# A spectral filter beside a 32-head attention: the filter's last stage computed for 321 of 640 columns, GpSimd joining the mirrored rest, and a planner that knows GpSimd's exclusion

## The chip, the cores and the metric

The program runs on one core of one Trainium2 chip. The metric is the device time of one execution in microseconds (us); the runs of the kernel before took 755.43, 756.69 and 756.99 us.

## What is computed

Two independent blocks on bf16 inputs; their outputs stand side by side (2048 rows, 640 + 640 columns).

```python
def _A_ref(x, w_r, w_i):            # x: 1 x 2048 x 640
    X = rfft2(x.astype(float32), axes=(-2, -1))      # 2048 x 321
    X = X * (w_r + 1j * w_i)
    return irfft2(X, s=(2048, 640)).astype(bfloat16)

def _B_ref(x, wqkv, wo):            # 32 heads of 20
    q, k, v = heads(x @ wqkv)
    p = softmax(q @ k.T * 20 ** -0.5)
    return (p @ v) @ wo
```

## The kernel before, in words

**Attention** has 32 units (512 queries by 4 heads), each of 64 score tiles of 128 x 512, 2048 tiles in all. TensorE (PE) writes score tiles to PSUM banks (L817). A tile then takes one of two ways:

- Two tiles at a time go to ScalarE (ACT), which takes the exponential of 1024 columns in one instruction (L1444).
- Four tiles make a batch for VectorE (DVE): it clamps each tile out of PSUM to an integer (`p1`, L972, one tile or two), and makes two shifted copies of the batch in SBUF (`p2`, L1020, and `p3`, L1019, 2048 columns each). The exponential is the sum of three terms. GpSimd (POOL) scales the value tile for one of them (`vs`, L1029; on DVE, L1031, before the folding below is done).

PE then multiplies with the values (`pv`, L1102): 4 matmuls for 4 tiles of ACT, 12 for a batch of DVE. At the end of a unit the sums are inverted and sent round through DRAM, and POOL normalises (`onorm`, L1154). The projections are L620, L649 and L698, transposes of the input L598, the output product L1248 and L1253. At the start DVE copies four padded weight blocks (`padw`, L559), without which the first projections cannot run, while POOL fills constants with memsets (L566 to L572).

**The filter** works on rows folded by symmetry. POOL folds the input early (`fold`, L1659 to L1666). Then PE runs four stages of matmuls in the gaps of the attention: S1 (L1772), S2 (L1855), S3 (L1959) and S4 (L2011), with DVE taking results out of PSUM. S4 makes the output: for each of 8 blocks of 128 rows, two halves of 320 columns and two sets T, six matmuls of 320 columns sum cosine and sine parts in one bank; DVE copies set 0 to `T1` (L2019) and adds and subtracts set 1 (L2030, twice) into the rows `s` and `s + 1024`, which are stored.

**The order** of every engine's instructions is fixed when the program is built. The class `KB` plays the program through with a price for each instruction (the numbers beside each operation, such as `exp_occ`), and writes down what each engine takes next: `try_act_fill` and `dve_fill` share the score tiles out between ACT and DVE as each comes free, `try_bg` puts projection and filter jobs into PE's gaps, `pick_dve` chooses DVE's next operation, `step_aux` POOL's and the DMA queue's. Filter jobs have release times that are spread between `FT0` = 200 us and `FT1` = 700 us in proportion to PE's price of the jobs ahead. `keep_warm` adds a dummy matmul (L1536) where PE would idle. On the chip the engines run these fixed orders and wait for each other by semaphores. In `put`, a DVE operation `p2` or `p3` that is begun while POOL is busy costs 44% of the overlap more.

## Time and profile before

| | |
|---|---|
| runs, median of 3 | 756.69 us (755.43 to 756.99) |
| profiled execution, first to last instruction | 759.9 us |
| PE / DVE / ACT / POOL busy | 722.7 / 678.2 / 723.8 / 206.7 us |
| exponentials on ACT | 774 of 1024 columns |
| mean granted TensorE clock | 0.994 |

The profiled execution has no other time of its own than its span; it lies 3.2 us over the median of the runs. Busy times of PE come from pipelined matmuls with modelled ends, so they say little of how near PE is to its peak. For ACT and DVE the busy share can be read as it stands.

### The profile page before, as it was taken

What the parts mean: (1) busy time and instruction counts of PE and PEld (TensorE: products, weight loads), DVE (VectorE), ACT (ScalarE), POOL (GpSimd) and SP (SyncE); (2) the same over time, 40 slices, a digit from 0 to 9 for tenths busy, and PEclk for the clock granted to TensorE, in tenths of its full rate; (3) what the DMA queues carried; (4) which work ended last, traced back from release to release, by engine and by line L of the source; (5) the groups of instructions that cost most, each with busy time, mean ns of one, the idle gap of its engine ahead of it and who ended that gap; (6) DMA issues with size and microseconds to landing.
All of it is one profiled execution on the core that took longest, in us unless ns stands there. A gap on an engine that the chain in (4) does not pass through costs nothing.

```text
span 759.9 us, 16458 instructions
## 1 busy us (share of the span) xinstructions
PE 722.7 (95%) x6520; PEld 232.3 (31%) x6565; DVE 678.2 (89%) x1172; ACT 723.8 (95%) x787; POOL 206.7 (27%) x253
## 2 busy tenths in 40 slices
PE   8998999999999999999999999999999999999997
PEld 4422232332322222232223323322222232333333
DVE  3599999989989899999989988999899999999895
ACT  5899999999999999999999989999999999999994
POOL 7296952111211022122331123212121222122110
PEclk9999999999999999999999989999999999999999
DMA  9023321202102116213120112103010012111101
GB/s 314 11 72 90 96 71 52 48 20 49 34 21 57 42 46 222 76 37 104 38 53 16 47 37 51 24 21 110 20 44 22 16 46 84 38 45 48 51 23 56
DMA packets 43503, 44.68 MB, mean 59 GB/s; under 512 B 16740, under 2 KB 36582, under 8 KB 43166
## 3 DMA queue, kind: packets, MB, share of 16 engines
q1 hardware_dynamic: 42654, 42.25, 18.9%
q0 software_dynamic: 768, 1.32, 0.7%
q8 instruction: 54, 0.88, 0.5%
q14 instruction: 27, 0.22, 0.1%
HBM read 28.47 MB, written 8.36 MB: 48 GB/s over the span
## 4 chain that ended last, share of the span: by engine, by line
PE 51%; ACT 38%; DVE 9%; issue 2%; DVEq 0%
ACT arena L1444 37%; PE ps L817 18%; PE ps L1102 14%; PE ps L649 5%; DVE arena L972 3%; PE ps L698 3%; PE ps L1855 3%; PE ps L1772 2%; DVE arena L1019 2%; PE ps L1248 2%; PE ps L2011 2%; PE ps L1959 2%; DVE arena L1020 1%; PE ps L620 1%; PE ps L578 1%
## 5 line engine op out<-in xcount | busy, mean ns | idle before, releaser
L1444 ACT ACTIVATE arena<-ps 128x1024 f16<-128x1024 f32 x774 | 716.6, 1092 | 17.6 <-PE ps L817 11.2
L972 DVE TENSOR_SCALAR arena<-ps 128x512 int16<-128x512 f32 (+1 forms) x490 | 330.8, 692 | 31.8 <-PE ps L817 30.4
L817 PE MATMUL ps<-arena 32*128 32x512 bf16 x2048 | 304.9, 386 | 13.6 <-ACT arena L1444 10.0
L1102 PE MATMUL ps<-arena 128*32 128x512 f16 x3048 | 240.9, 386 | 4.4 <-DVE arena L1019 2.1
L817 PEld LDWEIGHTS ps<-arena 32*128 32x128 bf16 x2048 | 75.1, 91 | 285.9 <-ACT arena L1444 255.9
L1029 POOL TENSOR_SCALAR arena<-arena 128x96 bf16<-128x96 bf16 x112 | 74.5, 669 | 250.6 <-PE ps L1102 245.7
L1019 DVE TENSOR_SCALAR arena<-arena 128x2048 int16<-128x2048 int16 x125 | 93.7, 750 | 5.5 <-PE ps L1102 5.1
L1154 POOL TENSOR_TENSOR arena<-arena 128x512 bf16<-128x512 f32 x30 | 40.6, 1353 | 204.8 <-DMA arena<-rd 204.7
L1020 DVE TENSOR_SCALAR arena<-arena 128x2048 int16<-128x2048 int16 x125 | 92.9, 743 | 1.5
L1102 PEld LDWEIGHTS ps<-arena 128*32 128x32 bf16 x3048 | 52.3, 94 | 104.2 <-issue 70.2
L649 PE MATMUL ps<-arena 128*128 128x512 bf16 x149 | 45.7, 383 | 4.2 <-issue 2.4
L1855 PE MATMUL ps<-arena 128*128 128x322 bf16 (+1 forms) x198 | 39.2, 311 | 3.3 <-DVE arena L1904 1.8
L2011 PE MATMUL ps<-arena 128*128 128x320 bf16 (+1 forms) x192 | 35.7, 302 | 0.1
L698 PE MATMUL ps<-arena 128*128 128x160 bf16 x320 | 32.2, 234 | 1.0 <-DVE arena L972 1.0
L1887 DVE TENSOR_TENSOR arena<-ps,arena 128x644 bf16<-128x644 f32 (+1 forms) x34 | 27.9, 821 | 4.1 <-PE ps L1855 2.3
L1959 PE MATMUL ps<-arena 128*128 128x512 bf16 (+3 forms) x123 | 29.9, 333 | 1.3 <-issue 1.3
L1248 PE MATMUL ps<-arena 128*128 128x320 bf16 (+1 forms) x152 | 28.2, 302 | 0.2 <-DVE arena L1887 0.2
L1133 DVE COPY arena<-ps 128x512 f32<-128x512 f32 (+1 forms) x33 | 22.0, 669 | 5.9 <-PE ps L1102 5.6
L698 PEld LDWEIGHTS ps<-arena 128*128 128x128 bf16 x320 | 21.1, 98 | 14.7 <-issue 11.1
L661 DVE TENSOR_SCALAR arena<-ps 128x512 bf16<-128x512 f32 x34 | 23.1, 678 | 0.1
L1772 PE MATMUL ps<-arena 128*128 128x512 bf16 x72 | 21.7, 383 | 1.0 <-issue 0.8
L1855 PEld LDWEIGHTS ps<-arena 128*128 128x128 bf16 (+1 forms) x198 | 14.9, 98 | 21.6 <-issue 10.8
(83 smaller groups left out, 369.9 us busy)
## 6 DMA issues: line engine op xcount, KB each, us to landing
arena<-rd SPq DMA_DIRECT2D x120, 64.0 KB
out_dram<-arena SPq DMA_DIRECT2D x32, 160.0 KB
arena<-in_A_x_dram SPq DMA_DIRECT2D x16, 160.0 KB
xs<-arena SPq DMA_DIRECT2D x16, 160.0 KB
arena<-xs SPq DMA_DIRECT2D x4, 640.0 KB
arena<-arena SPq DMA_DIRECT2D x105, 20.0 KB
arena<-ct SPq DMA_DIRECT2D x2, 1024.0 KB
arena<-ct SPq DMA_DIRECT2D x4, 512.0 KB
```

Source lines behind the costliest of these rows:

```text
L649: return lambda e: e.matmul(o, l, r_, start=(cc == 0), stop=(cc == 4))
L698: return lambda e: e.matmul(o, l, r_, start=st, stop=(c == 4), skip_group_check=True)
L817: return e.matmul(self.ps[:, bank, :], self.KT[32 * j:32 * j + 32, g, kt * 128:(kt + 1) * 128], self.QT[32 * j:32 * j + 32, g, qc * 512:(q ...
L972: return e.tensor_scalar(o, in_, 0.0, 31744.0, ALU.max, ALU.min)
L1019: self.dve_push([(lambda e, en: e.tensor_scalar(Ii, Ii, SH2, 0.0, ALU.subtract, ALU.max), occ, ik + pk, ik, [], "p3")], lambda: push(self. ...
L1020: ops = [(lambda e, en: e.tensor_scalar(Gi, Ii, SH1, 0.0, ALU.subtract, ALU.max), occ, ik, [("G", b)], [], "p2")]
L1029: self.pool_op(lambda e: e.tensor_scalar(vs, vi, W1, None, ALU.mult), 300.0, r=vr, w=vk, name="vs")
L1102: inst = e.matmul(self.ps[32 * j:32 * j + 32, bank, :], v_, p_, start=s_, stop=False, tile_position=(0, 32 * j), skip_group_check=True)
L1444: self.put("act", lambda e: e.activation(o, in_, AF.Exp, bias=ACT_BIAS, scale=ACT_SCALE), 0.8333 * 512 * n + 60.0, r=[("ps", b) for b in b ...
L1855: return lambda e: e.matmul(o, lhs, r_, start=st, stop=sp)
L1959: return lambda bank: (lambda e: e.matmul(ps[0:M, bank, lo_:hi_], l, rhs, start=st, stop=sp, skip_group_check=True))
L2011: return lambda e: e.matmul(o, l, r_, start=(n == 0), stop=(n == 5))
```

## The change

Four things are changed at once.

1. **S4.** Cosine sums (m = 0) and sine sums (m = 1) go to banks of their own, for columns 0 to 320 alone (`FBC` = 322 with padding). Three matmuls of 322 columns fill a bank instead of six of 320: 96 matmuls in place of 192. DVE's operations keep their number (16 copies to `T1`, 32 adds and subtracts) at 322 columns, but write f32 buffers `uw`. The columns from 321 to 639 mirror 319 to 1: there the cosine sum is the same and the sine sum has the other sign.
2. **join.** Four new POOL operations for each of the 8 row blocks: cosine plus sine for columns 0 to 320, cosine minus sine read backwards for 321 to 639, for each of two rows. 32 in all; the stores follow them.
3. **The planner's exclusion.** `plock` holds, for POOL and DVE, the end of the last operation of the list `PORT`. An operation of the list on one of the two starts, in the plan, only after that of the other has ended; `pick_dve` passes such an operation over if POOL holds the lock for over 100 ns more. The 44% rule is gone.
4. **Prices.** `exp` 913 to 905 ns for two tiles, `p2`/`p3` 632 to 600, `vs` 300 to 430, `onorm` 1600 to 1250, `fold` 1600, 1500, 440, 860, 1160 to 1360, 1460, 275, 820, 815.

```diff
-        if eng == "dve" and name in ("p2", "p3", "p4") and self.free["pool"] > st:
-            occ += min(self.free["pool"] - st, 1.8 * occ) * 0.44
+        port = name in self.PORT
+        if port and eng == "dve":
+            st = max(st, self.plock["pool"])
+        if port and eng == "pool":
+            st = max(st, self.plock["dve"])
         end = st + occ
+        if port:
+            self.plock[eng] = end
...
+    PORT = {"p2", "p3", "vs", "S2.evL", "padw", "onorm", "fold", "ms_vp", "ms_v1", "ms_k", "ms_q", "x24z", "wpad", "wz", "ms_sb", "join"}
...
+            if op[5] in self.PORT and self.plock["pool"] > self.now + 100.0:
+                continue
...
-        return 0.8333 * 512 * n + 60.0
+        return 0.8333 * 512 * n + 52.0
...
-            for half in range(2):
+            b2 = sc % 2
+            for m in range(2):
                 for T in range(2):
                     pe = []
-                    for n in range(6):
-                        lt, m = divmod(n, 2)
+                    for lt in range(3):
...
-                            r_ = self.G[0:M, lt, m, half * 320:(half + 1) * 320]
-                            return lambda e: e.matmul(o, l, r_, start=(n == 0), stop=(n == 5))
+                            r_ = self.G[0:M, lt, m, :]
+                            return lambda e: e.matmul(o, l, r_, start=(lt == 0), stop=(lt == 2))
...
+                                return lambda e, en: e.tensor_tensor(self.uw[b2][m][sgn], self.T1, ps[:, bank, 0:FBC], op)
...
+    def join(self, sc, b2):
+        za = ("z", "A", 3)
+        for sgn in range(2):
+            c, n = self.uw[b2][0][sgn], self.uw[b2][1][sgn]
+            y = self.yo[sgn]
...
+            self.pool_op((lambda y, c, n: lambda e: e.tensor_tensor(y[:, 0:321], c[:, 0:321], n[:, 0:321], ALU.add))(y, c, n), 817.0, r=r, w=[("ys", sc, sgn, 0)], name="join")
+            self.pool_op((lambda y, c, n: lambda e: e.tensor_tensor(y[:, 321:640], c[:, 319:0:-1], n[:, 319:0:-1], ALU.subtract))(y, c, n), 817.0, r=r, w=[("ys", sc, sgn, 1)], name="join")
```

The planner makes another order of the whole program from this. Lines of the changed kernel stand 10 to 15 lower (L1444 is L1456 there, L817 is L827, L2011 is L2025). Three places of the two orders follow; "x774" is a count of equal instructions in a row.

ACT's whole order before, from its first copy of a transposed block to the end of the attention:

```order
L604 COPY arena<-ps 128x3x256
L604 COPY arena<-ps 128x2x256
L604 COPY arena<-ps 128x3x256 x2
L604 COPY arena<-ps 128x2x256
L1444 ACTIVATE arena<-ps 128x1024 x774
```

And now:

```order
L614 COPY arena<-ps 128x3x256 x3
L614 COPY arena<-ps 128x2x256
L714 CAST arena<-ps 128x2x8x20
L614 COPY arena<-ps 128x3x256
L1456 ACTIVATE arena<-ps 128x1024 x782
```

Eight more exponentials stand on ACT, and so 16 score tiles fewer on DVE: its batches fall from 125 to 121, PE's `pv` matmuls from 3048 to 3016. PE's dummy matmuls rise from 32 to 47.

PE's start before, from its 11 warming matmuls to the first score tiles:

```order
L578 MATMUL ps<-arena 128x512 x11
L598 MATMUL ps<-arena 128x128 x20
L1536 MATMUL ps<-arena 128x512
L620 MATMUL ps<-arena 128x512 x10
L598 MATMUL ps<-arena 128x128 x20
L817 MATMUL ps<-arena 128x512 x4
```

And now:

```order
L588 MATMUL ps<-arena 128x512 x11
L608 MATMUL ps<-arena 128x128 x20
L630 MATMUL ps<-arena 128x512 x5
L608 MATMUL ps<-arena 128x128 x20
L630 MATMUL ps<-arena 128x512 x5
L708 MATMUL ps<-arena 128x160 x10
L630 MATMUL ps<-arena 128x512 x5
L608 MATMUL ps<-arena 128x128 x10
L827 MATMUL ps<-arena 128x512 x4
```

Ten value matmuls (L708), five more projection matmuls (L630) and ten transposes (L608) now stand ahead of the first scores. On DVE the four `padw` copies, in one row before, are apart, each behind other work.

POOL's order in the filter's last stage before (no operation of that stage is on POOL):

```order
L1029 TENSOR_SCALAR arena<-arena 128x96 x4
L1154 TENSOR_TENSOR arena<-arena 128x512
L1029 TENSOR_SCALAR arena<-arena 128x96 x5
L1154 TENSOR_TENSOR arena<-arena 128x512
```

And now, at the stage's start:

```order
L1039 TENSOR_SCALAR arena<-arena 128x96 x4
L2059 TENSOR_TENSOR arena<-arena 128x321
L2060 TENSOR_TENSOR arena<-arena 128x319
L2059 TENSOR_TENSOR arena<-arena 128x321
L2060 TENSOR_TENSOR arena<-arena 128x319
L1039 TENSOR_SCALAR arena<-arena 128x96
L1164 TENSOR_TENSOR arena<-arena 128x512
```

The joins come in fours between the `vs` operations. By the number of score tiles that PE has issued, the stage's matmuls stood between the tiles 1744 and 2035 and stand now between 1800 and 1951; S1 began at tile 823 and begins at 819, S3 ended at 1712 and ends at 1780. Between the first and last DVE add of the stage stand 16 `p2` and `p3` operations now.

## Rows read from the trace of the kernel before

**Rows 1.** The page's first two parts: busy time by engine, granted clock in 40 slices.
```profile
PE 722.7 (95%) x6520; PEld 232.3 (31%) x6565; DVE 678.2 (89%) x1172; ACT 723.8 (95%) x787; POOL 206.7 (27%) x253
...
PEclk9999999999999999999999989999999999999999
```
**Rows 2.** The page's fourth part: the chain that ended last, by engine.
```profile
PE 51%; ACT 38%; DVE 9%; issue 2%; DVEq 0%
```
**Rows 3.** Groups by line: busy us, mean ns of one | idle before, releasers.
```profile
L1444 ACT ACTIVATE arena<-ps 128x1024 f16<-128x1024 f32 x774 | 716.6, 1092 | 17.6 <-PE ps L817 11.2 <-PE ps L1102 4.6
...
L1019 DVE TENSOR_SCALAR arena<-arena 128x2048 int16<-128x2048 int16 x125 | 93.7, 750 | 5.5 <-PE ps L1102 5.1
L1020 DVE TENSOR_SCALAR arena<-arena 128x2048 int16<-128x2048 int16 x125 | 92.9, 743 | 1.5
...
L2011 PE MATMUL ps<-arena 128*128 128x320 bf16 (+1 forms) x192 | 35.7, 302 | 0.1
...
L1666 POOL TENSOR_TENSOR arena<-arena 128x319 bf16<-128x319 f32 x16 | 16.0, 1002 | 0.0
...
L2030 DVE TENSOR_TENSOR arena<-arena,ps 128x320 bf16<-128x320 f32 x32 | 15.2, 475 | 1.5 <-PE ps L2011 1.4
```
**Rows 4.** Timeline of ACT: start us, us, instruction [idle before, releaser].
```profile
13.78 14.77 ACT L1444 ACTIVATE arena<-ps 128x1024 f16<-128x1024 f32 x16 [0.48 <-PE ps L817]
29.59 5.61 ACT L1444 ACTIVATE arena<-ps 128x1024 f16<-128x1024 f32 x6 [1.04 <-PE ps L817]
37.48 8.36 ACT L1444 ACTIVATE arena<-ps 128x1024 f16<-128x1024 f32 x9 [2.28 <-PE ps L817]
...
637.24 55.10 ACT L1444 ACTIVATE arena<-ps 128x1024 f16<-128x1024 f32 x60 [0.21 <-PE ps L817]
...
739.08 8.40 ACT L1444 ACTIVATE arena<-ps 128x1024 f16<-128x1024 f32 x9
```
**Rows 5.** Timeline of PE and POOL from the start to the first scores.
```profile
8.44 0.39 PE L1536 MATMUL ps<-arena 128*128 128x512 bf16 x1 [0.60 <-ACT arena L604]
9.24 2.32 PE L620 MATMUL ps<-arena 128*128 128x512 bf16 x10 [0.40 <-ACT arena L604]
11.39 1.28 PE L598 MATMUL ps<-arena 128*128 128x128 bf16 x20
...
13.68 1.14 PE L698 MATMUL ps<-arena 128*128 128x160 bf16 x14
```
**Rows 6.** Timeline around 70 us: a `p2` beside a fold on POOL.
```profile
69.86 1.94 DVE L1020 TENSOR_SCALAR arena<-arena 128x2048 int16<-128x2048 int16 x1
69.86 1.39 POOL L1659 TENSOR_TENSOR arena<-arena 128x640 f32<-128x640 bf16 x1
...
71.86 0.62 PE L1102 MATMUL ps<-arena 128*32 128x512 f16 x8 [0.46 <-DVE arena L1020]
...
72.83 1.94 ACT L1444 ACTIVATE arena<-ps 128x1024 f16<-128x1024 f32 x2 [0.28 <-PE ps L817]
```
**Rows 7.** Timeline of DVE at 196 us: a `p2` with POOL at rest.
```profile
196.07 0.68 DVE L1020 TENSOR_SCALAR arena<-arena 128x2048 int16<-128x2048 int16 x1
```
**Rows 8.** Timeline of PE near 441 us: filter matmuls of 322 columns, and `pv`.
```profile
440.63 0.59 PE L1855 MATMUL ps<-arena 128*128 128x322 bf16 x3
...
441.48 0.61 PE L1102 MATMUL ps<-arena 128*32 128x512 f16 x8
...
444.13 0.83 PE L1102 MATMUL ps<-arena 128*32 128x512 f16 x12
...
458.40 1.00 PE L1855 MATMUL ps<-arena 128*128 128x322 bf16 x6
```
**Rows 9.** Windows of 40 us: busy PE, PEld, DVE, ACT, POOL (instructions), granted clock, DMA.
```profile
80.00:120.00 40.00, 37.77 (x375) 13.45 (x377) 37.87 (x63) 38.41 (x42) 24.47 (x28) 1.00 0.31 92
440.00:480.00 40.00, 37.29 (x299) 11.86 (x291) 33.79 (x54) 35.21 (x39) 11.57 (x12) 0.91 0.18 43
640.00:680.00 40.00, 39.70 (x381) 12.69 (x382) 38.25 (x70) 40.00 (x45) 8.21 (x11) 1.00 0.13 38
```

More of the change, by code (lines that the diff above doesn't have):

```diff
@@ L323, in __init__ @@
         self.cold = False
+        self.plock = {"pool": 0.0, "dve": 0.0}
         self.win = 0
@@ L424, in alloc_filter @@
         self.Z = a.bf(zB, 3 * 4 * 1024).rearrange("p (t m s) -> p t m s", t=3, m=4)
[L425 removed]
+        self.G = a.bf(zA, 3 * 2 * FBC).rearrange("p (t m d) -> p t m d", t=3, m=2)
         self.outB += [a.bf(o, 640) for o in (zC + 5888, zC + 7168)]
[L427 to L428 removed]
+        self.T1 = a.f32(zA + 3872, FBC)
+        self.uw = [[[a.f32(zA + 5184 + 5152 * i + 2576 * m + 1288 * s, FBC) for s in range(2)] for m in range(2)] for i in range(2)]
+        self.yo = [a.bf(zA + 15488 + 1280 * s, 640) for s in range(2)]
+        assert 15488 + 2560 <= 20608
     def at(self, t):
@@ L1153, in norm_dma @@
         pk = self.pack_keys(u - 1) if u else []
-        self.pool_op(lambda e: e.tensor_tensor(on, of, bc, ALU.mult), 1600.0, r=pk + [("bcu", u, j) for j in range(4)] + [("bc", j) for j in range(4)] + [("Of", b2)],
+        self.pool_op(lambda e: e.tensor_tensor(on, of, bc, ALU.mult), 1250.0, r=pk + [("bcu", u, j) for j in range(4)] + [("bc", j) for j in range(4)] + [("Of", b2)],
                      w=[("On",), ("Onu", u)] + al, name="onorm")
@@ L2012, in jobs_A @@
                         ks = [(z_, lt, 2 * T + m) for z_ in ("Z", "Zm", "Zr")] + [("G",), zr("A", 3), zr("B", 2), zr("D", 3)]
-                        if T == 1 and sc >= 2 and n == 0:
-                            ks += [("yout", sc - 2, 0), ("yout", sc - 2, 1)]
-                        pe.append((mk, 136.0, ks))
+                        pe.append((mk, 137.0, ks))
+                    post = None
                     if T == 0:
-                        def mkev(bank, half=half):
-                            in_ = ps[:, bank, 0:320]
-                            return lambda e, en: e.tensor_copy(self.T1[half], in_)
@@ L2020, in jobs_A, with mkev @@
-                        rk = [zr("A", 3)] + ([("yo", sc - 1, half, 1)] if sc else [])
-                        ev = [(mkev, 405.0, rk, [("T1", half), zr("A", 2)], [], False)]
-                        post = None
+                        def mkev(bank):
+                            return lambda e, en: e.tensor_copy(self.T1, ps[:, bank, 0:FBC])
+                        rk = [zr("A", 3)] + ([("uw", sc, 0)] if m else [("uw", sc - 1, 1)] if sc else [])
+                        ev = [(mkev, 402.0, rk, [("T1", sc, m), ("T1",), zr("A", 2)], [], False)]
@@ L2025, in jobs_A, with mkev, post @@
                         for sgn in range(2):
-                            def mkev(bank, half=half, sgn=sgn, sc=sc):
-                                in_ = ps[:, bank, 0:320]
-                                o = self.yo[sc % 2][sgn][:, half * 320:(half + 1) * 320]
+                            def mkev(bank, sgn=sgn, b2=b2, m=m):
                                 op = ALU.add if sgn == 0 else ALU.subtract
-                                return lambda e, en: e.tensor_tensor(o, self.T1[half], in_, op)
-                            ev.append((mkev, 408.0, [("T1", half), zr("A", 3)], [("yo", sc, half, sgn), zr("A", 2)], [("yob", sc % 2, sgn)], False))
-                        post = None
-                        if half == 1:
-                            def post(J, sc=sc):
-                                o = self.out[0]
-                                for sgn in range(2):
-                                    r0 = 128 * sc + 1024 * sgn
-                                    rows = o[r0:r0 + 128, 0:640]
-                                    self.dma(rows, self.yo[sc % 2][sgn], 163840, r=[("yo", sc, hh, sgn) for hh in range(2)] + [("yob", sc % 2, sgn)],
-                                             w=[("yout", sc, sgn)], name="st_A", is_out=True)
+                                return lambda e, en: e.tensor_tensor(self.uw[b2][m][sgn], self.T1, ps[:, bank, 0:FBC], op)
+                            rk = [("T1", sc, m), ("T1",), zr("A", 3)] + ([("ys", sc - 2, i, h) for i in range(2) for h in range(2)] if sc >= 2 else [])
+                            ev.append((mkev, 402.0, rk, [("uwk", sc, m, sgn), zr("A", 2)] + ([("uw", sc, m)] if sgn else []), [], False))
+                        if m == 1:
+                            def post(J, sc=sc, b2=b2):
+                                self.join(sc, b2)
                     add(Job("S4", 0.0, pe, ev, after=S3, post=post))
```

38 lines of the change are left out of this document (20 added, 18 removed).

## The prediction

> **What bounds the kernel now.** I read the page's busy times first, then the chain, the groups by line, and last ACT's timeline and three windows. Three engines are nearly full: PE 95%, ACT 95%, DVE 89%, POOL only 27% [rows 1]. PE's share is made of pipelined matmuls and shows no limit by itself. The chain that ended last runs over PE for 51% and ACT for 38% [rows 2], so it passes to and fro between the two. What tells them apart is ACT's own beat. In its longest unbroken row, 60 exponentials take 55.10 us [rows 4]; less the last one's 1.09 us [rows 3] that is 54.0 us for 59, or 0.915 us each. ACT's attention lasts from 13.78 us to 739.08 + 8.40 = 747.5 us [rows 4], 733.7 us. At the unbroken beat 774 exponentials need 773 x 0.915 + 1.09 = 708.4 us. So ACT loses 25.3 us, some 3%, over the whole run, and is the bound for the rest; 13.8 us lie before its first exponential and 12.4 us behind its last. Whatever the change does to PE, DVE and POOL reaches the time only through those 25.3 us, through the start and the end, or through the number of exponentials.
>
> Where the loss lies matters. In the window 640 to 680 us, inside the filter's last stage, ACT is busy 40.00 of 40 us [rows 9]: the stage that is cut in half costs ACT nothing there. In the window 80 to 120 us, where POOL still folds, ACT has 38.41 [rows 9]. In 440 to 480 us it has 35.21 while the granted clock is 0.91 in the mean, part of it at 1.2 GHz rather than 2.4 GHz [rows 9]; the page's strip shows this one dip only [rows 1].
>
> **The change, part by part.** The sum is made against the profiled execution, 759.9 us, and then set against the runs, whose median lies 3.2 us lower.
>
> *More exponentials: +7.3 us.* The new order has 782 for 774. 8 x 0.915 = 7.3 us on the engine that bounds, with nothing beside it. This is mostly the new price: at 905 ns for 913 the planner hands ACT 0.9% more for the same planned time. DVE, which loses the 16 tiles, is not the engine that ends last.
>
> *The start: +2.2 us, and 2.2 us back.* Before the first score PE now does ten value matmuls more (14 took 1.14 us, so 0.8), five more projection matmuls (10 took 2.32, so 1.2) and ten transposes (20 took 1.28, so 0.6), and one dummy less (0.39): 2.2 us together [rows 5]. The cause is that the plan keeps `padw` off POOL's memsets. In return that work isn't due later. ACT's second and third stretch begin after 1.04 and 2.28 us without work, waiting for scores [rows 4]; I take 2.2 of these 3.3 us as returned. Ends: nothing returned (+2.2), all returned (-1.1).
>
> *The last stage on PE: no gain in its own place, 3 us elsewhere, 1 us at the end.* Six matmuls of 322 columns take 1.00 us and three take 0.59 [rows 8], 0.137 us each; 96 fewer are 13.2 us. A `pv` of four matmuls costs 0.83 - 0.61 = 0.22 us [rows 8]; 32 fewer matmuls are 8 x 0.22 = 1.8 us. The 15 more dummies at a full matmul's 0.23 us [rows 5] take 3.5 back. PE has 11.5 us less to do, but the stage it leaves had 0.1 us of waiting in front of its matmuls [rows 3] and a full ACT [rows 9]. The gain can only come from the release times: S1 to S3 now stretch over 961 score tiles where they had 889, 8% thinner, so less of PE's work lies between two scores. Ends: 0, and 8 us, a third of ACT's loss; I take 3, nearer to 0 as the fully loaded window showed no loss. The stage's last matmul moves from 13 tiles before the end to 97 before it, so it no longer meets the last output product; I take 1 us of the 12.4 us tail, ends 0 and 2.
>
> *DVE in the last stage: 0.* Its 16 copies and 32 adds remain, two columns wider; an add took 475 ns [rows 3]. They now stand closer together, as the stage is shorter, and DVE takes fewer tiles there; that is already in the count of exponentials.
>
> *The joins: 0, at a price of 26 to 32 us on POOL.* The nearest row is the fold's operation on 319 columns with one side backwards, 1.0 us in the mean [rows 3], 16.0 us for 16 of them; 32 joins are 32 us by that row, 26 us by the plan's 0.817. POOL has some 550 us free [rows 1]. Behind a join wait the next join, a `vs` or an `onorm`; the stores after the joins end well before the attention does. By the mean row the joins cost nothing, since they lie beside other work. The Trainium skill, "Perfetto Trace Analysis", section "Optimizing Scalar/DVE Operations", says that GpSimd and VectorE share a port, so that moving operations between the two might not help; by that the joins would give their price to DVE, and this is the second rival below.
>
> *The exclusion: -6 us.* A `p2` beside a fold took 1.94 us: both began at 69.86, POOL's took 1.39 and the `p2` ended 0.55 us after it [rows 6]; with POOL at rest one takes 0.68 us [rows 7]. PE's next `pv` waited 0.46 us for it and ACT then had a gap of 0.28 [rows 6]. Over all, `p2` and `p3` take 743 and 750 ns in the mean [rows 3], so DVE loses 125 x (0.063 + 0.070) = 16.6 us to it. The new plan puts other DVE work into such moments. Ends: 16.6 us if every collision goes and every one had reached ACT; 0 if the real times drift so far from the plan that as many are made anew. I take 6, about a third, as the example passed 0.28 of its 1.26 us to ACT at once and more through the scores behind it. With `padw` the exclusion only costs; that is in the start.
>
> *The clock dip: 0.* It holds 4.8 us of lost ACT time [rows 9]. Nothing in the change speaks for or against it, and I leave it in the sum, with both ends (-4.8, or one more).
>
> The sum: 759.9 + 7.3 + 2.2 - 2.2 - 3 - 1 - 6 = 757.2 us of span, which is 2.7 us less than before; against the runs that is 756.7 - 2.7 = **754.0 us**, a gain of 0.4%.
>
> **The rivals.** A measurement of this kernel can tell 0.2% from no change, some 1.5 us, so faster means under 755.2 us and slower over 758.2.
>
> *ACT simply gets more to do.* Slower: the eight exponentials and the later start are sure, written in the order; what should pay for them is an estimate. If the exclusion and the thinner filter return nothing, the time is 756.7 + 7.3 + 2.2 = 766 us, or 764 with the start's share back. The place is ACT's whole row. The point from which it decides: fewer than 8 us returned of the 25.3 (9.5 us of cost less 1.5). For it speaks that ACT is full where PE's load is highest; against it that the collisions are visible, and that the plan's prices now match the rows (0.905 planned, 0.915 measured).
>
> *The joins take the port from DVE.* Slower: in the last stage there are 32 joins and 16 `p2`/`p3`. If each of the 16 waits for a whole join of about 0.9 us, DVE is 14 us late, by half of it 7 us; the stage is short and ACT must then wait for PE behind DVE: 756.7 - 2.7 + 7 = 761 us. It needs the plan's exclusion to fail in the real run, and the collisions to come in the stage whose tiles are the last to be made up. For it speaks that POOL is held for about half of that stage.
>
> *Nothing.* What is returned equals the 9.5 us of cost: 755.2 to 758.2 us. It needs only that my 12.2 us be 8 to 11.
>
> *More than I take.* All of the collisions' 16.6 us go instead of 6: 743 us; or the 6 stand and the clock dip stays away in every run: 749 us. Against it speaks that only some of the waits of DVE reach ACT.
>
> **How the numbers follow.** The forecast, 750 to 755.2 us, has 0.33; a larger gain 0.14; nothing 0.18; ACT's extra work alone 0.23; the port 0.12. So faster is 0.47, same 0.18, slower 0.35. The range runs from 745 us, between the two cases of the larger gain, to 766 us, where the first rival returns nothing at all; about 1 in 10 is left out on each side. My forecast is only the likeliest of cases of both signs; its own range is 750 to 755.2 us.
>
> **What would show it.** In the changed kernel's profile the group of exponentials should have 782 at the same beat, and its first one should start near 16 us. `p2` and `p3` should fall from 743 and 750 ns towards 700, most of all before 120 us; that would be the exclusion's step. If they stay, that step is wrong, and with it the gain. The windows from 300 to 600 us should show ACT nearer to 40 of 40; if they don't, the thinner filter returned nothing. Joins of 0.82 to 1.0 us, with no long `p2` beside them, would put the port's rival aside. What would make the prediction wrong at a stroke is a loss on ACT of 25 us as before, or a second dip of the granted clock.

## The result, and the profile after

| | before | changed |
|---|---|---|
| runs, median (17 of each, side by side) | 756.92 us (755.42 to 760.5) | 760.77 us (758.41 to 764.06) |
| ratio, 95% interval | | 1.0057 [1.0043, 1.0072] |
| profiled execution, span | 759.9 us [rows 1] | 759.0 us |

The changed kernel is slower by 0.57%, some 4 us. The forecast was 754.0 us, faster. The time lies in the stated range (745 to 766), but the change has the other sign.

One thing has to be known ahead of all else: the profiled execution of before holds a dip of the granted clock to the lower level (1.2 GHz), 6.8 us long, at 450.6 us, in the stretch of [rows 9], and its span plus the 1.8 us by which a time lies over its span makes 761.7 us, 4.8 over the median. In 18 of 29 runs of before (those beside the first four experiments) the mean granted clock was 0.999 or more, with a median of 755.85 us; in seven it was 0.996 or less, with 760.44. The profiled execution of the changed kernel has no dip; its span is 758.96 us and its time, 760.77 us, is the median of its runs. So the two spans may not be compared as they stand.

The page of the changed kernel, busy time by engine and granted clock:

```profile
PE 719.2 (95%) x6404; PEld 228.5 (30%) x6452; DVE 666.0 (88%) x1124; ACT 729.0 (96%) x796; POOL 230.0 (30%) x285
...
PEclk9999999999999999999999999999999999999999
```

ACT has 5.2 us more to do than before, DVE 12.2 less, POOL 23.3 more [rows 1]. The same page's groups by line (busy us, mean ns of one | idle before, releaser):

```profile
L1456 ACT ACTIVATE arena<-ps 128x1024 f16<-128x1024 f32 x782 | 721.1, 1111 | 9.7 <-PE ps L1112 5.4
...
L1164 POOL TENSOR_TENSOR arena<-arena 128x512 bf16<-128x512 f32 x30 | 40.5, 1351 | 195.0 <-DMA arena<-rd 195.0
L1029 DVE TENSOR_SCALAR arena<-arena 128x2048 int16<-128x2048 int16 x121 | 91.7, 761 | 3.0 <-PE ps L1112 2.5
L1030 DVE TENSOR_SCALAR arena<-arena 128x2048 int16<-128x2048 int16 x121 | 90.1, 745 | 1.2
...
L2059 POOL TENSOR_TENSOR arena<-arena 128x321 bf16<-128x321 f32 x16 | 14.6, 914 | 23.8 <-DVE arena L2039 23.0
```

The 782 exponentials stand there, and ACT waits less in front of them than before (9.7 us for 17.6 [rows 3]). `p3` (L1029) and `p2` (L1030) take 761 and 745 ns; they took 750 and 743 [rows 3]. That is the first step of the prediction that failed: the exclusion did not shorten them.

ACT's account, from the start times of all exponentials in both traces (the median distance of two is 904 ns in both; what a distance has beyond that counts as lost):

| us | before | changed | difference |
|---|---|---|---|
| first exponential starts | 13.8 | 16.6 | +2.8 |
| 774 and 782 exponentials at 0.904 | 699.7 | 706.9 | +7.2 |
| lost between them | 33.8 | 23.5 | -10.3 |
| from the last one's end to the end | 12.5 | 11.6 | -0.8 |

Of the 33.8 us, some 4.2 are the dip's: the four units of 64 score tiles in which it fell took 98.4 us, and 94.2 in experiment e3, where their order is the same. Without the dip 6.1 us are returned, not 10.3, and the account gives +3 us of the 3.9 us by which the medians differ. The rest of this document asks what kept the return so small.

By stretch, from PE's first score tile of a unit to that of another (read from PE's score matmuls; units have 64 tiles; "tail" is from the last score tile to the end; a unit starts 0.4 us before its first exponential, so a row sums to some 0.5 us over the span):

| us | first exponential | units 0-3 | units 4-27 | units 28-31 | tail |
|---|---|---|---|---|---|
| before | 13.8 | 99.1 | 544.4 (540 without the dip) | 89.1 | 14.0 |
| changed | 16.6 | 99.9 | 535.3 | 94.3 | 13.3 |

The start loses 2.8 us and the first units 0.8; the middle gains some 5; the last four units lose 5.2. The two places of loss show in the timelines. First the start of the changed kernel, POOL, DVE, PE and ACT (start us, us, instruction [idle before, releaser]):

```profile
6.36 0.95 POOL L580 MEMSET arena<- 128x1024 f32 x1
6.81 0.36 DVE L569 COPY arena<-arena 128x400 bf16<-128x400 bf16 x1 [3.93 <-DMA arena<-in_B_wqkv_dram]
...
11.69 0.96 POOL L580 MEMSET arena<- 128x1024 f32 x1
11.90 0.35 DVE L569 COPY arena<-arena 128x400 bf16<-128x400 bf16 x1
...
12.51 1.03 PE L630 MATMUL ps<-arena 128*128 128x512 bf16 x4 [0.90 <-DVE arena L569]
...
16.59 24.86 ACT L1456 ACTIVATE arena<-ps 128x1024 f16<-128x1024 f32 x27
```

The second `padw` copy (L569) comes 5 us after the first, and PE's projections wait for it. (First exponentials vary by about 1 us from run to run: 15.4 to 16.6 us in the changed kernel and the four experiments e1, e2, e4 and e9, which start like it, 12.7 to 13.8 in the twelve profiles of the old start; between the means lie 2.9 us.) The copies took 0.35 us each with a memset running beside them, and the memsets 0.95. In the old order all four took 1.33 in one row beside memsets of 0.95:

```profile
6.00 1.33 DVE L559 COPY arena<-arena 128x400 bf16<-128x400 bf16 x4 [3.13 <-DMA arena<-in_B_wqkv_dram]
6.37 0.95 POOL L570 MEMSET arena<- 128x1024 f32 x1
```

So there was no collision to avoid here. The second place lies near 680 us, in the filter's last stage; the windows of before and of the changed kernel (busy PE, PEld, DVE, ACT, POOL, clock, DMA):

```profile
680.00:700.00 20.00, 19.52 (x185) 6.62 (x183) 19.27 (x36) 20.00 (x23) 3.77 (x4) 1.00 0.17 48
```
```profile
680.00:700.00 20.00, 18.64 (x158) 5.98 (x156) 19.76 (x36) 16.57 (x19) 13.41 (x15) 1.00 0.20 65
```

ACT, full before, loses 3.4 of 20 us. The timeline of the changed kernel there:

```profile
674.26 0.87 POOL L2059 TENSOR_TENSOR arena<-arena 128x321 bf16<-128x321 f32 x1 [2.63 <-DVE arena L2039]
...
675.09 0.86 POOL L2060 TENSOR_TENSOR arena<-arena 128x319 bf16<-128x319 f32 x1
...
675.90 0.88 POOL L2059 TENSOR_TENSOR arena<-arena 128x321 bf16<-128x321 f32 x1
...
676.73 0.86 POOL L2060 TENSOR_TENSOR arena<-arena 128x319 bf16<-128x319 f32 x1
...
677.56 0.45 POOL L1039 TENSOR_SCALAR arena<-arena 128x96 bf16<-128x96 bf16 x1
...
679.21 1.28 DVE L1030 TENSOR_SCALAR arena<-arena 128x2048 int16<-128x2048 int16 x2
...
680.81 0.68 DVE L1029 TENSOR_SCALAR arena<-arena 128x2048 int16<-128x2048 int16 x1
...
681.55 1.66 PE L1112 MATMUL ps<-arena 128*32 128x512 f16 x24 [0.28 <-DVE arena L1029]
...
683.14 1.44 PE L2025 MATMUL ps<-arena 128*128 128x322 bf16 x9
683.26 3.77 ACT L1456 ACTIVATE arena<-ps 128x1024 f16<-128x1024 f32 x4 [2.94 <-PE ps L1112]
```

Four joins and a `vs` stand in one row on POOL up to 678.0. No `p2` and no `p3` runs beside them; two `p2` follow in one piece at 679.21 and the `p3` at 680.81. Behind that `p3` PE has 24 `pv` matmuls in one row, and ACT waits 2.94 us. None of these DVE instructions is slow (the `p2` take 0.64 us each, the `p3` 0.68); the order itself is bad.

Between the two places the sign that the prediction had named did come. From 300 to 600 us ACT was busy 291.2 of 300 us before, the dip included, and is busy 299.3 now:

```profile
300.00:600.00 300.00, 287.54 (x2506) 86.47 (x2522) 279.21 (x484) 291.21 (x315) 67.79 (x89) 0.99 0.16 47
```
```profile
300.00:600.00 300.00, 289.27 (x2539) 87.04 (x2551) 276.36 (x471) 299.27 (x327) 65.88 (x89) 1.00 0.16 45
```

### The profile page after: what moved, and what is told of

Its sections match the earlier page's. It is cut to its first block, busy times and chain, and to the rows that moved or that the text cites. A ratio compares the mean times of both kernels' runs of the same rounds, so it can differ in the third digit from the quotient of the medians.

```text
span 759.0 us, 16222 instructions
## 1 busy us (share of the span) xinstructions
PE 719.2 (95%) x6404; PEld 228.5 (30%) x6452; DVE 666.0 (88%) x1124; ACT 729.0 (96%) x796; POOL 230.0 (30%) x285
## 3 DMA queue, kind: packets, MB, share of 16 engines
q1 hardware_dynamic: 42654, 41.77, 18.7%
## 5 line engine op out<-in xcount | busy, mean ns | idle before, releaser
L1456 ACT ACTIVATE arena<-ps 128x1024 f16<-128x1024 f32 x782 | 721.1, 1111 | 9.7 <-PE ps L1112 5.4
L982 DVE TENSOR_SCALAR arena<-ps 128x512 int16<-128x512 f32 (+1 forms) x455 | 317.3, 715 | 38.9 <-PE ps L827 36.2
L827 PE MATMUL ps<-arena 32*128 32x512 bf16 x2048 | 309.2, 384 | 19.4 <-ACT arena L1456 13.3
L827 PEld LDWEIGHTS ps<-arena 32*128 32x128 bf16 x2048 | 76.4, 91 | 289.5 <-ACT arena L1456 262.0
L1029 DVE TENSOR_SCALAR arena<-arena 128x2048 int16<-128x2048 int16 x121 | 91.7, 761 | 3.0 <-PE ps L1112 2.5
L1030 DVE TENSOR_SCALAR arena<-arena 128x2048 int16<-128x2048 int16 x121 | 90.1, 745 | 1.2
L708 PE MATMUL ps<-arena 128*128 128x160 bf16 x320 | 32.2, 234 | 0.0
L1258 PE MATMUL ps<-arena 128*128 128x320 bf16 (+1 forms) x152 | 28.7, 302 | 0.0
L708 PEld LDWEIGHTS ps<-arena 128*128 128x128 bf16 x320 | 21.2, 98 | 13.9 <-issue 12.8
L714 DVE CAST arena<-ps 128x320 bf16<-128x320 f32 x31 | 15.2, 489 | 9.4 <-PE ps L708 9.1
L2059 POOL TENSOR_TENSOR arena<-arena 128x321 bf16<-128x321 f32 x16 | 14.6, 914 | 23.8 <-DVE arena L2039 23.0
```

Of the source, the lines that this page charges most:

```text
L708: return lambda e: e.matmul(o, l, r_, start=st, stop=(c == 4), skip_group_check=True)
L827: return e.matmul(self.ps[:, bank, :], self.KT[32 * j:32 * j + 32, g, kt * 128:(kt + 1) * 128], self.QT[32 * j:32 * j + 32, g, qc * 512:(q ...
L982: return e.tensor_scalar(o, in_, 0.0, 31744.0, ALU.max, ALU.min)
L1029: self.dve_push([(lambda e, en: e.tensor_scalar(Ii, Ii, SH2, 0.0, ALU.subtract, ALU.max), occ, ik + pk, ik, [], "p3")], lambda: push(self. ...
L1030: ops = [(lambda e, en: e.tensor_scalar(Gi, Ii, SH1, 0.0, ALU.subtract, ALU.max), occ, ik, [("G", b)], [], "p2")]
L1258: return lambda e: e.matmul(o, ot[0:M, c, qb * 128:(qb + 1) * 128], self.wo[0:M, c, half * 320:(half + 1) * 320], start=(c == 0), stop=(c ...
```

## The experiments

Seventeen kernels were run. My theory after the result: the exclusion, as planned, returns nothing on DVE, and what it moves (the start, the `p2` beside the joins) costs the time. The first rival: ACT simply has eight exponentials more to do. The second: joins hold the port and delay DVE in the real run. All ratios are to before on the same chip; its own median went from 756.9 to 758.9 us from chip to chip, so a median is to be compared through its ratio.

| kernel | median us | ratio, 95% interval |
|---|---|---|
| e1_join_tiny | 759.06 | 1.0030 [1.0008, 1.0052] |
| e2_planner_only | 762.73 | 1.0069 [1.0042, 1.0096] |
| e3_stage_only | 759.78 | 1.0049 [1.0020, 1.0077] |
| e4_stage_spread | 761.09 | 1.0045 [1.0021, 1.0069] |
| e5_no_exclusion | 758.50 | 0.9985 [0.9961, 1.0009] |
| e6_start_kept | 757.39 | 0.9976 [0.9948, 1.0004] |
| e7_start_kept_old_stage | 759.29 | 0.9996 [0.9972, 1.0020] |
| e8_start_kept_old_stage_old_exp | 759.34 | 1.0002 [0.9971, 1.0033] |
| e9_join_not_excluded | 758.66 | 1.0024 [1.0008, 1.0041] |
| e10_late_start_alone | 760.95 | 1.0051 [1.0031, 1.0071] |
| e11_start_and_fold_free | 757.99 | 0.9997 [0.9977, 1.0016] |
| e12_start_fold_join_free | 757.35 | 1.0003 [0.9984, 1.0022] |
| e13_start_kept_join_free | 760.43 | 1.0027 [1.0006, 1.0047] |
| e14_prices_alone | 764.52 | 1.0078 [1.0051, 1.0105] |
| e15_late_start_in_before | 762.13 | 1.0052 [1.0029, 1.0076] |
| e16_old_rule_new_stage_prices | 754.21 | 0.9954 [0.9931, 0.9977] |
| e17_as_e16_old_exp_price | 756.45 | 0.9979 [0.9958, 1.0000] |

### The joins, the stage and the planner apart

e1, joins of one column in the same order (all but two of an output row's 640 filter columns are left out):

```diff
-e.tensor_tensor(y[:, 0:321], c[:, 0:321], n[:, 0:321], ALU.add)
+e.tensor_tensor(y[:, 0:1], c[:, 0:1], n[:, 0:1], ALU.add)
-e.tensor_tensor(y[:, 321:640], c[:, 319:0:-1], n[:, 319:0:-1], ALU.subtract)
+e.tensor_tensor(y[:, 321:322], c[:, 319:320], n[:, 319:320], ALU.subtract)
```

> The changed kernel in the same order, but each of the 32 joins works on one column, so three quarters of the filter's output columns are left out. Theory A (the written order holds the loss of the last stage: DVE is crowded there by the copies and adds of a stage that now lasts 58 us instead of 101): 760 to 761 us, and ACT's gap of 2.9 us near 680 us stays. Rival B (the joins' real time on the port that POOL shares with DVE makes p2 and p3 late): 756.5 to 758 us, the gap at 680 us gone.

A join took 215 ns in the mean for 902, and the kernel stayed slower than before by 0.30%. The last four units took 93.3 us for 94.3, and ACT's gap near 680 us remained, 2.94 us as in the changed kernel. By the two ratios (1.0030 for 1.0057) the joins' own time is worth some 2 us, by the units 1; the intervals overlap.

e2 is the changed kernel with the old stage, as the diff shows; e3 is the kernel before with the new stage and its joins (the same diff the other way), old prices and the 44% rule:

```diff
-            for m in range(2):
+            for half in range(2):
...
-                    for lt in range(3):
+                    for n in range(6):
+                        lt, m = divmod(n, 2)
...
```

> The exclusion and the new prices with the old last stage (192 matmuls, no joins). 780 exponentials, the late start stays. Theory A: the start (2.8 us) and six exponentials (5.5 us) cost 8 us and the collisions avoided return some 5 us; without the crowded last stage 757 to 759 us. Rival C (the planner's part is the gain and the last stage alone the loss): 750 to 755 us. Rival D (the planner's part is the whole loss, the last stage a gain): 762 us or more.

> The new last stage with joins, under the old planner and the old prices. 774 exponentials, the start as before. Theory A: the start and the exponentials cost nothing, the stage's crowding costs 2 to 4 us and the freed PE time returns 1 to 3 us: 755 to 759 us. Rival C (the last stage alone is the loss): 760 us or more. Rival D (the stage is a gain by itself): 750 to 754 us.

Each alone is slower. In e2 the last four units took 87.8 us, 1.3 less than before, but the tail 22.5 us. Its PE timeline ends with

```profile
746.52 9.16 PE L2021 MATMUL ps<-arena 128*128 128x320 bf16 x66
```

that is, 66 of the old stage's 192 matmuls stand behind the attention. The profiled execution of e3 has a dip at 80.8 us, so its stretches show less; its 1.0049 says that the new stage brings nothing under the old prices. Planner and stage are not two terms that add up: each sets what the other is worth.

e4, release times with the new stage at double weight:

```diff
+        wt = lambda J: (2.0 if J.name == "S4" else 1.0) * sum(c[1] for c in J.pe)
```

> The changed kernel with the release times of the filter's jobs reckoned as if the last stage cost PE twice its price, so that it lies over about as many score tiles as before the change. Still 782 exponentials. Theory A: the gap near 680 us and the loss of 4 us in the last units go, the filter's earlier stages get denser again: 757 to 759 us. Rival B (joins and the port): no change, 760 to 762 us.

The plan came out the same on every engine, so the release times do not bind there. As a time it is only a second measurement of the changed kernel, 1.0045. But it shows that the release times are not what spread the filter's stages over more score tiles.

### Without the exclusion, and with the start kept

e5 empties the list; e6 takes only the start's operations from it; e7 and e8 build on e6 with the old stage and then the old price of an exponential:

```diff
-    PORT = {"p2", "p3", "vs", "S2.evL", "padw", "onorm", "fold", "ms_vp", "ms_v1", "ms_k", "ms_q", "x24z", "wpad", "wz", "ms_sb", "join"}
+    PORT = set()
```
```diff
-    PORT = {"p2", "p3", "vs", "S2.evL", "padw", "onorm", "fold", "ms_vp", "ms_v1", "ms_k", "ms_q", "x24z", "wpad", "wz", "ms_sb", "join"}
+    PORT = {"p2", "p3", "vs", "S2.evL", "onorm", "fold", "x24z", "wpad", "wz", "ms_sb", "join"}
```

> The changed kernel with an empty list PORT: new prices, new last stage and joins, no exclusion in the plan. 774 exponentials and the start as before the change. Theory A (the exclusion in the plan brings the eight exponentials and the late start, 10 us, and returns 5 us of stall): 755.5 to 758 us. Rival C (the exclusion is a gain and the rest of the change the loss): 761 us or more. p2 and p3 should be longer than in the changed kernel if the exclusion had avoided collisions.

> The changed kernel, but padw and the memsets at the start are not in PORT. 776 exponentials, PE's order up to the first score as before the change. Theory A: 2.8 us of start and 6 x 0.904 = 5.4 us of exponentials come back, 752.5 to 756 us, first exponential at 13 to 14.5 us. Rival E (the late start is made good by work done ahead, as the prediction had it, so that only the exponentials matter): 755.5 to 757.5 us.

> The same start, the exclusion and the new prices with the old last stage (192 matmuls, no joins). 778 exponentials; the last matmul of the stage stands 7 score tiles before the end, where it stood behind the end in the planner-only kernel. Theory A: without the tail of 20.8 us that kernel had, and with stalls of 20 us as it had: 751 to 754 us. Rival C (the new last stage is the gain): slower than the kernel with the start kept and the new stage by 2 us or more.

> As the run before, and the price of the exponential back at 913 ns. 774 exponentials. Theory A (the number of exponentials counts for what they take): 778 - 774 = 4 fewer, 3.6 us less unless stalls grow: 749 to 752 us. Rival F (the number does not matter, since ACT's stalls fill the difference): within 1 us of the run before.

Both e5 and e6 are quicker than the changed kernel, with intervals that lie apart from its own. Groups by line of e5, without any exclusion:

```profile
L1029 DVE TENSOR_SCALAR arena<-arena 128x2048 int16<-128x2048 int16 x125 | 94.8, 761 | 1.7 <-PE ps L1112 1.2
L1030 DVE TENSOR_SCALAR arena<-arena 128x2048 int16<-128x2048 int16 x125 | 92.7, 742 | 1.5
...
L2059 POOL TENSOR_TENSOR arena<-arena 128x321 bf16<-128x321 f32 x16 | 16.5, 1034 | 22.6 <-DVE arena L2039 18.4
```

`p2` and `p3` take 742 and 761 ns, where they take 745 and 761 with it. POOL's operations are shorter with the exclusion (the join 914 for 1034 ns, the second fold 1455 for 1633), but POOL is not the engine that is waited for. With the start kept, the rest of the exclusion (e6) is not to be told from none (e5): neither harm nor good shows. My theory had put e6 at 752.5 to 756 us, e7 at 751 to 754 and e8 at 749 to 752; all three came out slower. e7 and e8 differ by four exponentials (778 and 774) and not in time; the number of exponentials alone decides nothing.

### Which part of the list

e9 takes only `join` from the list; e10 leaves only the start's five names in it; e11 is e6 without `fold`, e12 also without `join`, e13 is e6 without `join`. For instance e10:

```diff
-    PORT = {"p2", "p3", "vs", "S2.evL", "padw", "onorm", "fold", "ms_vp", "ms_v1", "ms_k", "ms_q", "x24z", "wpad", "wz", "ms_sb", "join"}
+    PORT = {"padw", "ms_vp", "ms_v1", "ms_k", "ms_q"}
```

> The changed kernel with join taken out of PORT: the joins still run, but the plan no longer passes p2 and p3 over while one is under way. 782 exponentials and the same order of PE up to the last stage. Theory A2 (ACT's gap of 2.9 us near 680 us was written into the order: four joins and a vs in a row made the plan pass over two batches' p2, so that the next unit's values could not be multiplied and the ring of exponentials filled): the gap goes, the last four units take 90 to 92 us for 94.3, the ratio to before is 1.001 to 1.004. Rival G (DVE is simply full in that stage): the ratio stays at 1.005 to 1.007.

> PORT holds only padw and the memsets of the start: the late start without any exclusion afterwards. 772 exponentials; to be held against the kernel without exclusion (774 exponentials, ratio 0.9985). Theory A: the first exponential 2.5 to 3 us later, of which little comes back: ratio 1.000 to 1.003 in spite of two exponentials fewer. Rival E (the work done ahead pays the late start back, as the prediction had it): 0.996 to 0.999.

> As the kernel with the start kept (776 exponentials, ratio 0.9976), and fold taken out of PORT too, so that the plan no longer passes p2 and p3 over for POOL's folding. 772 exponentials. Theory A: the exclusion moved tiles to ACT in the first units for collisions that cost less than the exponentials; 4 x 0.9 = 3.6 us less, less what the collisions take, ratio 0.993 to 0.997. Rival H (the collisions with the folding cost as much as the exponentials): 0.997 to 1.000, with more stall in the first four units.

> As the run before, with join taken out of PORT as well; 770 exponentials. If theories A and A2 hold, the best of all, ratio 0.990 to 0.996. Rival H: as the run before or slower, with longer p2 and p3 in the last stage.

> The changed kernel with the start kept and join not excluded, the two edits that paid by themselves (776 exponentials). If they add up: 0.9976 - 0.003 = 0.994 to 0.997. Rival (the gap near 680 us was an accident of one order, and the kernel with the start kept had no such gap): 0.997 to 0.999, as the kernel with the start kept alone.

PE's order in e9 is the changed kernel's up to the last stage, and there its window reads

```profile
680.00:700.00 20.00, 18.59 (x167) 5.65 (x167) 19.30 (x36) 19.28 (x22) 12.76 (x15) 1.00 0.18 60
```

ACT has 19.28 us for 16.57, the last four units take 92.3 us for 94.3, and the kernel is 0.33% nearer to before (1.0024, the intervals just apart). So in this order it was the plan's exclusion of the joins that wrote the gap, not the joins' work. It is a matter of this one order: e6 excludes the joins too and has no such gap, ACT is busy 59.8 of 60 us there:

```profile
660.00:720.00 60.00, 56.88 (x515) 16.63 (x513) 56.77 (x107) 59.83 (x66) 33.47 (x41) 1.00 0.18 57
```

e10 took 1.0051 and e5 0.9985, and they differ by the start's five names only. But this 0.7% is not the late start's alone. In all twelve runs of e10 the mean granted clock was 0.997 or less, in six of e5's twelve 0.999 or more; e10's profile has two dips, one of them at 12.8 us, ahead of its first exponential at 18.7 us. How much of the 0.7% is the clock's stays open, and e10's stretches aren't used. e11 and e12, which my theory had at 0.997 or below, took before's time and can't be told from e6: with the start kept, no worth of the folds' exclusion shows. e13 speaks against a simple sum: taking `join` out of e6 made it slower, 1.0027 for 0.9976. In its trace nine `p2` or `p3` ran beside a join and lost 3.0 us (two and 0.6 in e6), and the last four units took 90.4 us for 87.6. There the joins did take time from DVE. That this made the kernel slow isn't shown: in e5 ten lost 4.4 us beside joins, and it took 0.9985.

### Prices, the late start and the old rule in the kernel before

e14 is before with the new prices alone; e15 is before with the 44% rule and the exclusion of the start's five operations; e16 is before with the new stage and the new prices, the 44% rule kept and no exclusion; e17 is e16 with the old price of an exponential. e16's diff to the changed kernel:

```diff
-        port = name in self.PORT
-        if port and eng == "dve":
-            st = max(st, self.plock["pool"])
-        if port and eng == "pool":
-            st = max(st, self.plock["dve"])
+        if eng == "dve" and name in ("p2", "p3", "p4") and self.free["pool"] > st:
+            occ += min(self.free["pool"] - st, 1.8 * occ) * 0.44
...
-            if op[5] in self.PORT and self.plock["pool"] > self.now + 100.0:
-                continue
```

> The kernel before with the new prices alone: old last stage, no exclusion, the 44% rule kept. 772 exponentials, the start as before; the filter's stages stand later (S3 ends at tile 1814 for 1712) and part of the last stage is left behind the last score. Theory (the prices bring the gain of the middle units): units 4 to 27 take 535 to 537 us for some 539, but the tail grows: ratio 0.998 to 1.006. Rival (the prices bring nothing there): units 4 to 27 at 538 us or more.

> The kernel before with the late start alone: padw and the memsets exclude each other in the plan, all else old (774 exponentials, old prices and last stage). Theory A (the late start costs what it delays, 2.5 to 3 us, and nothing comes back): ratio 1.003 to 1.005. Rival E (the work done ahead pays it back): 0.999 to 1.001.

> The kernel before with the new last stage, the joins and the new prices: the 44% rule kept, no exclusion. 774 exponentials, start as before. Theory R (the old rule served the first units better than the exclusion): 98 to 100 us in units 0 to 3, no tail of 22 us as with the prices alone, ratio 0.991 to 0.997. Rival: 101 us or more in the first units as in the kernel without exclusion, ratio 0.998 or more.

> As the run before with the exponential's price at 913 ns; 772 exponentials; the last stage ends 96 score tiles before the end for 55. Theory R: 98 to 100 us in units 0 to 3, ratio 0.991 to 0.998. If the number of exponentials mattered by itself this would be 1.8 us faster than the run before; I expect the two within 2 us.

e15: the late start costs the old kernel 0.52% too, though its first four units take 96.9 us for 99.1 and the stretch up to their end closes only 0.7 us late. The rest comes due at the end: its PE timeline closes with

```profile
751.49 3.44 PE L2023 MATMUL ps<-arena 128*128 128x320 bf16 x24
```

24 matmuls of the old stage behind the attention, and a tail of 16.3 us for 14.0.

e14: with the new prices alone the middle took 536.2 us for 540, a dip of 3.4 us included, but the tail 23.1 us: 72 matmuls of the old stage stand behind the attention. With the new stage beside them (e16) the middle took 534.4 us and the tail 12.3, and the kernel beats both, with 0.9954. e17, with two exponentials fewer, is not better but 2.2 us slower in the median; their intervals overlap. ACT's timeline of e16 at the start, and its windows over the folds and over the last stage:

```profile
13.40 14.77 ACT L1446 ACTIVATE arena<-ps 128x1024 f16<-128x1024 f32 x16 [0.48 <-PE ps L819]
```
```profile
60.00:120.00 60.00, 56.88 (x533) 18.67 (x537) 57.50 (x91) 57.64 (x63) 39.43 (x44) 1.00 0.30 86
...
660.00:720.00 60.00, 57.31 (x498) 17.58 (x499) 58.80 (x107) 59.77 (x66) 34.14 (x39) 1.00 0.18 58
```

And the same windows of the changed kernel:

```profile
60.00:120.00 60.00, 58.30 (x506) 19.21 (x511) 44.99 (x70) 59.25 (x65) 36.66 (x42) 1.00 0.31 89
...
660.00:720.00 60.00, 55.97 (x487) 17.25 (x489) 59.09 (x108) 55.92 (x61) 35.33 (x43) 1.00 0.19 62
```

While POOL folds, DVE has 45.0 us of work in the changed kernel where e16 has 57.5 (without any exclusion e5 has 54.4, with the start kept e6 has 51.6); ACT is nearly full there, 59.3 of 60 us, and can't take more. In the last stage ACT has 55.9 us where e16 has 59.8.

## Why the prediction was wrong

Four kernels lead from before to the changed one, each a step from the one ahead of it. The new stage, joins and prices with the old rule and the old start (e16) took 0.9954 of before; without the 44% rule (e5) 0.9985; with the exclusion, but the start kept (e6) 0.9976; with the start's names too (the changed kernel) 1.0057. So the stage and the prices gained 0.5%, the exclusion returned nothing that can be told from none, and the loss came with the rule that was dropped (0.3%, intervals that overlap) and with the late start (0.8%, intervals that lie apart).

**What bounds.** ACT's beat held: 904 ns between two exponentials in both kernels, and the account by start, number, loss and tail closes. The prediction had read 0.915 us off one long row, and so ACT's loss before as 25.3 us where it was 33.8. The sum of before's row (759.9) was another matter: "The clock dip: 0" left 4.2 us in a loss that the change was to draw on, though the median of the runs, 4.8 us under that execution's own time, showed that most runs had no such loss.

**"More exponentials: +7.3 us."** At ACT's beat they are 7.2 us. But that is no term by itself: kernels with 770 (e12), 774 (e8) and 778 (e7) exponentials took 1.0003, 1.0002 and 0.9996 of before. An exponential more mostly fills a wait that ACT would have had: e9 has twelve more than e12, 10.8 us, and lost 21.3 us between them where e12 lost 33.0. Nor did the eight come from the new price, as the prediction had it: the prices alone give 772 (e14), without the exclusion there are 774 (e5), with the start kept 776 (e6), and the start's names bring six.

**"The start: +2.2 us, and 2.2 us back."** The first half measured 2.8 us. The second half failed: two pairs that differ only in the exclusion of the start's operations show the start alone at +0.5% (before to e15) and +0.8% (e6 to the changed kernel), 4 to 6 us; a third (e5 to e10, +0.7%) has the clock in it. The two gaps of ACT behind the start, which I took as the place where it comes back, did close (27 exponentials in one row from 16.59 us), and e15's first units did gain 2.2 us; but what was gained there was lost behind it: in e15 24 matmuls stood at the end, and the changed kernel's last four units took 94.3 us for e6's 87.6. This is the largest of the failed steps.

**"The exclusion: -6 us."** Nothing came. Of all `p2` and `p3` over 760 ns I counted, in both traces, which POOL operation lay beside them and what they took beyond 685 ns:

| beside | fold | `onorm` | `vs` | join | sum, us |
|---|---|---|---|---|---|
| before | 15: 6.9 us | 9: 6.4 | 12: 1.8 | - | 15.1 |
| changed | 7: 4.3 us | 11: 8.1 | 10: 1.8 | 3: 1.5 | 15.8 |

(One of 0.1 us beside another operation is in the last sum.) The folds' collisions fell from 15 to 7, as meant. `onorm` took their place. It starts when a transfer lands (195 us of its waiting stand to `rd` in its group above), and the plan's moment is not the chip's:

```profile
670.36 1.27 POOL L1164 TENSOR_TENSOR arena<-arena 128x512 bf16<-128x512 f32 x1
670.42 1.76 DVE L1030 TENSOR_SCALAR arena<-arena 128x2048 int16<-128x2048 int16 x1
```

The prediction named this end ("0 if the real times drift so far from the plan that as many are made anew") and gave it too little. Nor does the time follow these collisions. Counted in the same way, their sum was 12.0 us in e2 (1.0069), 12.9 in e6 (0.9976), 19.5 in e16 (0.9954) and 21.0 in e3 (1.0049). That a third of DVE's loss reaches ACT was drawn from one example, and no run bears it out. That POOL's operations got shorter is shown by the second fold, before and in the changed kernel:

```profile
L1660 POOL TENSOR_TENSOR arena<-arena 128x640 f32<-128x640 bf16 x8 | 13.4, 1678 | 0.1
```
```profile
L1672 POOL TENSOR_TENSOR arena<-arena 128x640 f32<-128x640 bf16 x8 | 11.6, 1455 | 0.1
```

The old 44% rule, which I priced at nothing, was worth something: kernels with it (before, e14 to e17) take 97 to 100 us for the first four units; those without it and with the early start (e5 to e8, e12, e13) 101.3 to 102.8, with the exclusion or without (e3 and e11 are left out, as a dip fell there). e16 and e5 differ by this rule alone, and e16 is ahead, 0.9954 for 0.9985, though the intervals overlap. In runs with a mean clock of 0.999 or more e16 took 752.0 to 752.3 us and e5 757.0 to 758.9, on chips where before had medians of 755.9 and 758.0 in such runs. That leaves some 4 us for the rule, a rough figure, as before took 754.8 to 760.9 us in such runs on e5's chip.

**"The last stage on PE: -3 elsewhere, -1 at the end."** The tail fell by 0.8 us, as said. The 3 us elsewhere are not the stage's: e3 has the stage and no gain, e2 and e14 have the shorter middle without it. The way to them, the release times, was wrong as well: with the old stage (e2) S1 to S3 lie between tiles 819 and 1780 just as in the changed kernel, with the new stage under the old planner (e3) between 823 and 1733, and e4's other release times moved nothing. Mostly it is the planner's rules and prices that spread them. What the stage does is what the prediction put at 1 us: with half the matmuls it is done before the attention's end. That is worth over 10 us of tail where the old stage comes late (23.1 in e14, 12.3 in e16).

**"The joins: 0."** By their own time nearly so: 1 to 2 us by e1, so the second rival was small. Its 761 us came nearest to the measured time, but by luck: only three of the long `p2` and `p3` ran beside a join, and lost 1.5 us. What I left out is the plan's reaction to the joins: passing over `p2` while four joins stand in a row wrote the gap near 680 us, 2 us of the last units by e9.

The first rival, "ACT simply gets more to do", was right in its condition: it was to decide if fewer than 8 us were returned, and 6 were. Half of its reason holds, the late start. The other half was not the cause: e7 has four of the eight exponentials more, and before's time.

**Left open.** The middle units differ by some 4 us between kernels with the same new prices and no dip (539.5 us in e7, 535.2 in e5). They go with how far the filter lags. Units 28 to 31 begin with tile 1792. Where S3's last matmul stands at tile 1780 or behind it (the changed kernel, e1, e2, e4 and e9 at 1780, e5 at 1807, e16 at 1814), the middle took 534.4 to 535.4 us; where it stands before (e7 at 1709, e8 at 1712, e3 at 1733, e13 at 1746, e11 and e12 at 1761), 537.5 to 541.9 (kernels with a dip in these units are left out). So the 5 us that the changed kernel gains in the middle look like work put off to its last units, which took 5.2 us more, some 2 of them by the gap near 680 us. No run was made to show it. And e13 shows that the parts of the list don't add up.

## What to carry to other kernels

When a planner writes the order, an edit of its rules is paid or earned through the whole written order: count what the two orders have at the first and the last work of the bounding engine, and don't credit a cause in between that the chip's real times can undo. A planned exclusion is worth trying only for operations whose start the plan knows, whose collision a trace shows, and whose delay is shown to reach the bounding engine; here the copies and memsets at the start didn't collide, `onorm`, which waits for a transfer, did not start when the plan had it, and the fastest kernel lost more to collisions than before (19.5 us for 15.1). And before a sum is made against one profiled execution, set that execution against the median of the runs, and take out what only it has.

## What the runs showed of the hardware

- The granted clock falls to the lower level, 1.2 GHz, now and then, mostly in the midst of an even load, and not in the same place of the same program each time: the profiled execution of e4, whose order is the changed kernel's, has dips at 655 and 689 us, that of the changed kernel has none. A dip of 10.2 us in e10 at 500.9 us, its window:

```profile
500.00:520.00 20.00, 19.48 (x139) 5.33 (x139) 15.53 (x27) 15.23 (x17) 1.77 (x4) 0.74 0.04 10
```

PE was as busy in it as ever (19.48 of 20 us) while ACT lost 4.8 us.

- GpSimd and VectorE collide by the kind of operation, not whenever both work: a `p2` beside an `onorm` took 1.76 us for 0.68, but a `padw` copy of 128 x 400 elements beside a memset took 0.35 us, as the last one did with POOL at rest, and the memset its 0.95. The Trainium skill, "SBUF — State Buffer", section "Who interferes with whom", says that the two share a pair of ports under an exclusive lock, and that a copy or `tensor_scalar` of VectorE takes it only where its operands meet the conditions of a faster mode. The first pair agrees with that; for the second, no run here shows whether the copy ran in such a mode.
- The joins read one side backwards at no price of their own: 319 columns with reversed reading took 890 ns in the mean, 321 forwards 914:

```profile
L2060 POOL TENSOR_TENSOR arena<-arena 128x319 bf16<-128x319 f32 x16 | 14.2, 890 | 0.0
```
